# A linear-attention block and two MLPs on one core: the first block's attention in float32 products, wider query loads, and the lower parts on another engine

## The chip, the core and the metric

One Trainium2 chip, of which the program uses one core. Its engines run side by side, each in its own program order: TensorE (PE, with its weight loads as PEld), VectorE (DVE), ScalarE (ACT), GpSimd (POOL) and SyncE (SP), which here issues nearly all DMAs. The metric is the device time of one execution in microseconds (us); lower is better.

## The reference, cut to what matters

```python
# q, k, v: (8, 8, 576, 64) float32; g_norm: (64,) float32
kv  = einsum('bhsd,bhse->bhde', k, v)
out = einsum('bhsd,bhde->bhse', q, kv)
rms = sqrt(mean(out * out, axis=-1, keepdims=True) + 1e-06)
x   = out / rms * g_norm                 # then (B, S, H*D) = 4608 tokens x 512
x   = max(0.01 * (x @ w_in), x @ w_in) @ w_out          # 512 -> 2048 -> 512
return max(x @ moe2_w_in, 0) ** 2 @ moe2_w_out           # 512 -> 2048 -> 512
```

The four weights arrive as float64, read as pairs of 32-bit words.

## The kernel before

**Precision.** A float32 operand is split into an upper part, rounded to the engine's short float32 form (`F32R`, an ACT copy), and a lower part, the rest (a subtraction). A product of two split operands is three matmuls: upper x upper, upper x lower, lower x upper. A plain `F32` product is one call of the program; for it the trace has two matmul records.

**Blocks.** 4608 tokens are 9 blocks `j` of 512. Attention prepares the input of block `j` as four head pairs `p` of two 64-wide heads, each 128 partitions of `x`. A batch has 576 tokens, so block 0 lies in batch 0 and block 1 takes its first 64 tokens from it too. The steps of a pair:
- `kv` (`do_kv`, L338): k^T v for both heads from raw tiles, then the split into `kv_t`.
- `a` (`stage_a`, L376): four transposes of the raw queries, then the split (ACT L382, DVE L383).
- `b` (`stage_b`, L386): the product with kv (L396 to L398: three matmuls for each batch that the block touches), then square and copy (ACT L403, L404) and the split of the square (DVE L405, POOL L406).
- `s` (`stage_s`, L411): the mean of squares over a head, a product with a constant matrix `ones`, upper part (L414) and then lower part (L415).
- `c` (`stage_c`, L419): the reciprocal root (ACT L424, L425) and three DVE steps (L426, L429, L432); the last one also needs `gneg`, which comes from `g_norm` (`load_g`, L713).
- `d` (`stage_d`, L437): the split of x, upper by ACT L440, lower by POOL L441.

**First GEMM.** A slot is one `gemm1(j, m)` (L476): 12 matmuls of 128x512 on column group `m` of the first weight, 16 slots a block, 144 in all. `leaky` (L491) takes the result out of PSUM on ACT into a tile of a small pool (`hp`) and a DMA stores it. Weights are made from the raw words by `scale` (ACT L172, DVE L173 and L176), `join` (DVE L186 and L190) and `w` (`split_w`, ACT L202, POOL L203). Three are made in the prologue, the other 13 one a slot during block 0. From slot 20 on the other three weight matrices are made in the same way, split on POOL (L259) and stored.

**Order.** The program is a list written out by hand; each engine keeps to it. The prologue has attention of block 0 with a step for each pair; then, in each slot, weight work comes first, then the GEMM, then the attention steps of block `j+1`: pair `p` starts every four slots, `b` two slots behind `a`, `s` and `c` two further, `d` one further. The order inside a slot is `("s", "c", "b", "a", "d", "kv")`.

**Loads and buffers.** `pump` (L946) issues loads on SP's queue in the order in which the program will use them, as far as buffers allow: 8 units for raw k, v and weights (a pair of k and v counts 2), 3 raw query tiles. It runs once at the start and after each step that frees a buffer, so what it issues stands on SP's queue ahead of a DMA that a later step issues. `g_norm` is loaded on ACT's queue, in the step behind `a` and `kv` of the prologue's step 0. Big tiles take numbered slots (45) from a first-in-first-out list. PSUM has 8 banks; in the prologue `at_tile` goes round them, so its 16th tile, the mean of squares of pair 3, takes bank 0, which the first GEMM takes next.

**Afterwards** come the second GEMM of the first MLP and both of the second MLP (L608, L672), from operands and weights re-read from DRAM.

Of the kernel before, what the change touches and what calls it, by code (L numbers as in the profile page):

```python
# [10 lines left out]
F32 = mybir.dt.float32  # L11
# [7 lines left out]
def tile_linear_attention_two_mlps(  # L19
# [26 lines left out]
    nc = tc.nc  # L46
# [16 lines left out]
    TB = 512  # L63
    EPS = 1e-6
    LD_BUFS, Q_BUFS, KV_BUFS = 8, 3, 6
# [23 lines left out]
    NBIG = 45  # L89
# [7 lines left out]
    hp = ctx.enter_context(tc.tile_pool(name="hp", bufs=4))  # L97
# [225 lines left out]
    def load_kv(b, p):  # L323
        tiles = []
        for n, x in enumerate((k, v)):
# [3 lines left out]
            for r, c in SCH:  # L329
                nc.sync.dma_start(  # L330
# [7 lines left out]
    def do_kv(b, p):  # L338
# [22 lines left out]

    def load_q(i, p):
        a = qp.tile([P, TB // P, P], F32, tag="q", name=f"q_raw{i}_{p}")
        for r in range(TB // P):
            t0, o = i * TB + r * P, 0
            while o < P:
                b, s = divmod(t0 + o, S)
                n = min(P - o, S - s)
                nc.sync.dma_start(
                    out=a[o:o + n, r, :].rearrange("p (h d) -> p h d", h=2),  # L370
                    in_=q[b, 2 * p:2 * p + 2, s:s + n, :].rearrange("h s d -> s h d"),
                )
                o += n
        q_raw[i, p] = a

    def stage_a(i, p):  # L376
        a = q_raw.pop((i, p))
        ps = at_tile(TB, f"qtps{i}_{p}")
        for r in range(TB // P):
            nc.tensor.transpose(ps[:, r * P:(r + 1) * P], a[:, r, :], ident)  # L380
# [5 lines left out]
    def stage_b(i, p):  # L386
# [4 lines left out]
        while o < TB:  # L391
# [3 lines left out]
            c = slice(o, o + n)  # L395
            nc.tensor.matmul(out=ps[:, c], lhsT=t[:, 0, :], rhs=hi[:, c], start=True, stop=False)  # L396
# [14 lines left out]
    def stage_s(i, p):  # L411
        sqo, slot, sqs, slot2 = sq_t.pop((i, p))
        ps = at_tile(TB, f"ssps{i}_{p}")
        nc.tensor.matmul(out=ps, lhsT=ones, rhs=sqs[:, 0], start=True, stop=False)  # L414
        nc.tensor.matmul(out=ps, lhsT=ones, rhs=sqs[:, 1], start=False, stop=True)  # L415
        give_big(slot2)
# [20 lines left out]
    def stage_d(i, p):  # L437
# [3 lines left out]
        nc.gpsimd.tensor_tensor(out=xl, in0=osb, in1=f32(xh), op=ALU.subtract)  # L441
# [11 lines left out]
    def attention_steps(j, pace, a, b_, c, d):  # L453
# [5 lines left out]
        for p in range(NP):  # L459
# [7 lines left out]
            add(at0 + c, "s", j, p)  # L467
# [252 lines left out]
    with tc.manual_schedule():  # L720

        prog = [("const",), ("x", 0)]
        steps = attention_steps(0, 1, 0, 1, 2, 3)
        jobs = [(0, m, 0) for m in range(NM)]
        for at0 in (2, 3, 4):
# [4 lines left out]
        for u in sorted(steps):  # L730
            order = ("b", "a", "s", "c", "d", "kv", "gn", "scale", "join", "w")
# [15 lines left out]
        for w in ((0, 1), (1, 0), (1, 1)):  # L747
            z, (a, b, c) = ("S", ("A11", "A12", "A22")) if LEFT[w] == 0 else ("T", ("B11", "B21", "B22"))
            for n in range(NPAIR):
# [3 lines left out]
                for st in (  # L753
# [6 lines left out]
                    ])  # L760
        n0, n1 = NM + 4, NM * NB - 12
# [116 lines left out]
        for s in range(len(slots)):  # L878
# [5 lines left out]
            order = ("s", "c", "b", "a", "d", "kv")  # L884
# [15 lines left out]
        def drop_pairs(ps):  # L900
# [10 lines left out]
            "a": stage_a, "b": stage_b, "s": stage_s, "c": stage_c, "d": stage_d, "mlp": spare.clear,  # L911
# [26 lines left out]

        pump()
# [38 lines left out]
```

## Time and profile before

| | |
|---|---|
| time, median of 3 runs | 1647.82 us (1647.33 to 1648.06) |
| profiled execution: time | 1646.02 us |
| profiled execution: span, first to last instruction | 1644.2 us |
| first GEMM: first matmul, last matmul ends | 41.7 us, 559.4 us |
| first GEMM, block 0 ends | 109.2 us |
| PE busy over the span | 1586.1 us (96%) |
| DVE, ACT, POOL busy | 1219.0, 768.1, 254.9 us |

The times are from the span's start. A busy PE is not a PE at its peak, since matmuls overlap; where the speed matters, it is read from the distance between starts.

### The profile page before, as it was taken

What the parts mean: (1) busy time and instruction counts of PE and PEld (TensorE: products, weight loads), DVE (VectorE), ACT (ScalarE), POOL (GpSimd) and SP (SyncE); (2) the same over time, 40 slices, a digit from 0 to 9 for tenths busy, and PEclk for the clock granted to TensorE, in tenths of its full rate; (3) what the DMA queues carried; (4) which work ended last, traced back from release to release, by engine and by line L of the source; (5) the groups of instructions that cost most, each with busy time, mean ns of one, the idle gap of its engine ahead of it and who ended that gap; (6) DMA issues with size and microseconds to landing.
All of it is one profiled execution on the core that took longest, in us unless ns stands there. A gap on an engine that the chain in (4) does not pass through costs nothing. (4 is left out here: it accounts for less than half of the span.)

```text
span 1644.2 us, 27915 instructions
## 1 busy us (share of the span) xinstructions
PE 1586.1 (96%) x10504; PEld 1424.0 (87%) x10504; DVE 1219.0 (74%) x1867; ACT 768.1 (47%) x1439; POOL 254.9 (16%) x272
## 2 busy tenths in 40 slices
PE   4999999999999999999999999999999999999999
PEld 3778777777777899999999988888888999999999
DVE  5967777777775378888778888747877787777776
ACT  4566555665565334444444454424444444444443
POOL 3444454454554000000000000000000000000000
PEclk7999999999999999999999999999999999999999
DMA  8677989989987954444335645584449833333442
GB/s 217 197 200 251 322 280 284 314 287 305 328 283 245 407 183 135 135 133 135 129 129 180 230 160 170 182 289 153 161 157 318 334 132 129 129 131 135 134 129 84
DMA packets 249447, 338.45 MB, mean 206 GB/s; under 512 B 55264, under 2 KB 180192, under 8 KB 249312
## 3 DMA queue, kind: packets, MB, share of 16 engines
q1 hardware_dynamic: 249152, 336.67, 61.5%
q8 instruction: 83, 1.36, 0.3%
q14 instruction: 52, 0.43, 0.1%
q10 hardware_dynamic: 160, 0.00, 0.0%
HBM read 198.18 MB, written 138.41 MB: 205 GB/s over the span
## 5 line engine op out<-in xcount | busy, mean ns | idle before, releaser
L481 PE MATMUL hps<-xh,w 128*128 128x512 f32 x1152 | 374.7, 397 | 8.4 <-DVE sqo L426 6.2
L481 PEld LDWEIGHTS hps<-xh,w 128*128 128x128 f32 x1152 | 217.7, 189 | 56.9 <-DVE sqo L426 6.7
L481 PE MATMUL hps<-xl,w 128*128 128x512 f32 x576 | 226.4, 393 | 0.8 <-POOL xl L441 0.8
L481 PEld LDWEIGHTS hps<-xl,w 128*128 128x128 f32 x576 | 109.2, 190 | 23.1 <-POOL xl L441 1.9
L493 ACT ACTIVATE h<-hps 128x512 f32<-128x512 f32 x144 | 85.0, 592 | 32.7 <-DMA g<-h 27.5
L587 DVE TENSOR_TENSOR h_C<-aps,u 128x512 f32<-128x512 f32 x72 | 49.5, 688 | 54.6 <-PE aps L608 33.1
L173 DVE TENSOR_SCALAR w_raw<-w_raw 128x512 uint32<-128x512 uint32 x64 | 48.8, 762 | 32.4 <-ACT wt L172 32.3
L587 DVE TENSOR_TENSOR u<-bps,p 128x512 f32<-128x512 f32 x72 | 49.5, 687 | 25.9 <-ACT p L618 12.9
L426 DVE SCALAR_TENSOR_TENSOR sqo<-ssps,sqo 128x512 f32<-128x512 f32 x36 | 24.9, 691 | 55.9 <-ACT sqo L425 55.0
L406 POOL TENSOR_TENSOR sqs<-sqo,sqs 128x512 fp32r<-128x512 f32 x36 | 49.2, 1366 | 85.9 <-DVE sqs L405 79.7
L190 DVE SCALAR_TENSOR_TENSOR wt<-wt,w_raw 128x512 uint32<-128x512 uint32 x64 | 58.1, 907 | 2.2
L441 POOL TENSOR_TENSOR xl<-sqo,xh 128x512 fp32r<-128x512 f32 x36 | 48.4, 1345 | 60.5 <-ACT xh L440 51.5
L618 ACT ACTIVATE p<-aps 128x512 f32<-128x512 f32 x36 | 21.3, 591 | 71.7 <-PE aps L608 71.7
L176 DVE SCALAR_TENSOR_TENSOR w_raw<-w_raw 128x512 uint32<-128x512 uint32 x64 | 53.0, 827 | 2.2
L608 PE MATMUL aps<-op_B21h,w 128*128 128x512 f32 (+1 forms) x160 | 52.2, 375 | 1.5 <-ACT p L618 1.5
L608 PE MATMUL bps<-op_T4h,w 128*128 128x512 f32 (+1 forms) x160 | 51.2, 369 | 0.6 <-DVE u L587 0.6
L608 PE MATMUL aps<-op_B22h,w 128*128 128x512 f32 (+1 forms) x160 | 51.2, 369 | 0.4 <-DVE h_C L587 0.4
L608 PE MATMUL bps<-op_T3h,w 128*128 128x512 f32 (+1 forms) x160 | 51.0, 368 | 0.0
L608 PE MATMUL bps<-op_T2h,w 128*128 128x512 f32 (+1 forms) x160 | 51.0, 368 | 0.0
L608 PE MATMUL aps<-op_B11h,w 128*128 128x512 f32 (+1 forms) x160 | 51.0, 368 | 0.0
L608 PE MATMUL aps<-op_T1h,w 128*128 128x512 f32 (+1 forms) x160 | 51.0, 368 | 0.0
L625 ACT ACTIVATE h_C<-aps 128x512 f32<-128x512 f32 x36 | 21.6, 599 | 62.1 <-issue 31.1
(1408 smaller groups left out, 4193.5 us busy)
## 6 DMA issues: line engine op xcount, KB each, us to landing
g_raw<-g SPq DMA_DIRECT2D x144, 512.0 KB, 5.6
w<-w SPq DMA_DIRECT2D x84, 512.0 KB, 6.6
g<-h SPq DMA_DIRECT2D x144, 256.0 KB, 5.7
g<-h_C SPq DMA_DIRECT2D x144, 256.0 KB, 2.5
w_raw<-in_moe_w_in_dram SPq DMA_DIRECT2D x32, 512.0 KB, 6.2
w_raw<-in_moe_w_out_dram SPq DMA_DIRECT2D x32, 512.0 KB, 5.8
w<-whS SPq DMA_DIRECT2D x64, 256.0 KB, 5.3
x_raw<-x SPq DMA_DIRECT2D x32, 512.0 KB, 6.2
```

The costliest lines, as they stand in the source:

```text
L173: nc.vector.tensor_scalar(out=upper, in0=upper, scalar1=0x80000000, scalar2=None, op0=ALU.bitwise_and)
L176: nc.vector.scalar_tensor_tensor(out=lower, in0=lower, scalar=29, in1=upper, op0=ALU.logical_shift_right, op1=ALU.bitwise_or,)
L190: nc.vector.scalar_tensor_tensor(out=t, in0=t, scalar=3, in1=lower, op0=ALU.logical_shift_left, op1=ALU.bitwise_or,)
L406: nc.gpsimd.tensor_tensor(out=sqs[:, 1], in0=sqo[:, 0], in1=f32(sqs[:, 0]), op=ALU.subtract)
L426: nc.vector.scalar_tensor_tensor(out=z, in0=ps, scalar=EPS, in1=z, op0=ALU.add, op1=ALU.mult)
L441: nc.gpsimd.tensor_tensor(out=xl, in0=osb, in1=f32(xh), op=ALU.subtract)
L481: nc.tensor.matmul(out=ps, lhsT=w[:, wh, c * P:(c + 1) * P], rhs=x_t[j][xh, c // 2][0][:, c % 2, :], start=(c == 0 and y == 0), stop=(c == ...
L493: nc.scalar.activation(out=h, in_=h_ps.pop((j, m)), func=AF.Prelu, alpha=0.01)
L587: nc.vector.tensor_tensor(out=t, in0=x, in1=y, op=ALU.add)
L608: nc.tensor.matmul(out=ps[:, p], lhsT=w[:, wh, c, :], rhs=t[xh][:, c, :], start=(fresh and p == 0 and c == 0 and y == 0), stop=(p == len(p ...
L618: nc.scalar.activation(out=p1, in_=ps, func=AF.Copy)
L625: nc.scalar.activation(out=h, in_=ps, func=AF.Relu)
```

## The change

- In block 0, kv stays in plain float32 (`kvf`, copied out by DVE), the queries are not split, and L396 to L398 become one float32 product. The split of kv that block 1 still needs is made later (`kvs`, slot 0).
- In blocks 0 and 1 the mean of squares is one float32 product of the unsplit square.
- From block 2 on the product of the square's lower part moves to a step of its own, `t`, one slot behind `s`; `c` moves with it, and the whole chain starts a slot earlier. In a slot, `a` now comes in a slot ahead of `c`.
- x's lower part is made by DVE in place of POOL, and so is the lower part of the first weight up to slot 16 (`relieve`, step `lo`).
- A query tile holds four consecutive tokens a partition: one DMA per head and batch. Four query tiles in place of three, 10 load units in place of 8, 5 `hp` tiles in place of 4, 44 big slots in place of 45.
- In the prologue, v of pairs 1 to 3 of batch 0 is loaded on ACT's queue, and `g_norm` on SP's. Weights 0 to 2 come one to two steps later in the order. Constants are set in another order.

```diff
-    LD_BUFS, Q_BUFS, KV_BUFS = 8, 3, 6
+    LD_BUFS, Q_BUFS, KV_BUFS = 10, 4, 6
-    NBIG = 45
+    NBIG = 44
+    PLAIN_SS = 2
-    hp = ctx.enter_context(tc.tile_pool(name="hp", bufs=4))
+    hp = ctx.enter_context(tc.tile_pool(name="hp", bufs=5))
+    kvf, kvf_slot = take_big([P, NP, 2, P], F32, "kvf")
+    kvf_t = [kvf[:, p, 0] for p in range(NP)]
+    lo_engine = [nc.vector]
+    def relieve():
+        lo_engine[0] = nc.gpsimd
...
-        nc.gpsimd.tensor_tensor(out=hl[:, 1], in0=t, in1=f32(hl[:, 0]), op=ALU.subtract)
+        lo_engine[0].tensor_tensor(out=hl[:, 1], in0=t, in1=f32(hl[:, 0]), op=ALU.subtract)
...
-                nc.sync.dma_start(
+                (nc.scalar if n and b == 0 and p else nc.sync).dma_start(
...
+        if b == 0:
+            for h in range(2):
+                r = slice(h * D, (h + 1) * D)
+                nc.vector.tensor_copy(out=kvf_t[p][r, r], in_=ps[r, r])
+            return
...
+    def split_kv(p):
+        t = kv_t[p]
+        nc.scalar.activation(out=t[:, 0], in_=kvf_t[p], func=AF.Copy)
+        nc.vector.tensor_tensor(out=t[:, 1], in0=kvf_t[p], in1=f32(t[:, 0]), op=ALU.subtract)
+        if p == NP - 1:
+            give_big(kvf_slot)
...
     def load_q(i, p):
-        a = qp.tile([P, TB // P, P], F32, tag="q", name=f"q_raw{i}_{p}")
...
+        a = qp.tile([P, QT, 2, D], F32, tag="q", name=f"q_raw{i}_{p}")
+        o = 0
+        while o < TB:
+            b, s = divmod(i * TB + o, S)
+            n = min(TB - o, S - s)
+            for h in range(2):
                 nc.sync.dma_start(
+                    out=a[o // QT:(o + n) // QT, :, h, :],
+                    in_=q[b, 2 * p + h, s:s + n, :].rearrange("(t c) d -> t c d", c=QT),
                 )
+            o += n
...
-            nc.tensor.transpose(ps[:, r * P:(r + 1) * P], a[:, r, :], ident)
+        by_c = ps.rearrange("f (t c) -> f c t", c=QT)
+        for c in range(QT):
+            nc.tensor.transpose(by_c[:, c, :], a[:, c].rearrange("p h d -> p (h d)"), ident)
+        if i == 0:
+            t, slot = take_big([P, 2, TB], F32, f"qf{i}_{p}")
+            nc.scalar.activation(out=t[:, 0], in_=ps, func=AF.Copy)
...
+            if i == 0:
+                nc.tensor.matmul(out=ps[:, c], lhsT=kvf_t[p], rhs=hi[:, c], start=True, stop=True)
...
+        if i < PLAIN_SS:
+            sq_t[i, p] = (sqo, slot, None, None)
+            return
...
+        if i < PLAIN_SS:
+            nc.tensor.matmul(out=ps, lhsT=onesf, rhs=sqo[:, 0], start=True, stop=True)
+        else:
+            nc.tensor.matmul(out=ps, lhsT=ones, rhs=sqs[:, 0], start=True, stop=False)
+        ss_t[i, p] = (sqo, slot, ps, sqs, slot2)
+    def stage_t(i, p):
+        sqo, slot, ps, sqs, slot2 = ss_t.pop((i, p))
+        if sqs is not None:
+            nc.tensor.matmul(out=ps, lhsT=ones, rhs=sqs[:, 1], start=False, stop=True)
+            give_big(slot2)
         ss_t[i, p] = (sqo, slot, ps)
...
-        nc.gpsimd.tensor_tensor(out=xl, in0=osb, in1=f32(xh), op=ALU.subtract)
+        nc.vector.tensor_tensor(out=xl, in0=osb, in1=f32(xh), op=ALU.subtract)
...
-            nc.scalar.dma_start(
+            nc.sync.dma_start(
                 out=gneg[h * D:(h + 1) * D, :], in_=g_norm.rearrange("(d o) -> d o", o=1)
...
-        for at0 in (2, 3, 4):
+        for at0 in (3, 5, 6):
...
+        for p in range(NP):
+            put(0, "kvs", p)
+        put(NM, "lo")
...
-                at0, pace = (s - 4, 4) if j else (s, 4)
+                at0, pace = (s - 5, 4) if j else (s, 4)
-                lags = (2, 4, 5) if j else (1, 2, 3)
+                lags = (2, 4, 5, 6) if j else (1, 2, 2, 3)
...
-            order = ("s", "c", "b", "a", "d", "kv")
+            order = ("s", "t", "c", "b", "a", "d", "kv", "kvs")
```

## Rows read from the trace of the kernel before

**Rows 1.** Windows: us; busy (instructions) of PE, PEld, DVE, ACT, POOL; clock; DMA.
```profile
0.00:41.70 41.70, 18.31 (x116) 12.34 (x116) 22.86 (x38) 19.38 (x38) 13.93 (x24) 0.78 0.80 215
41.70:109.20 67.50, 63.08 (x351) 48.42 (x352) 59.83 (x88) 41.01 (x80) 33.14 (x23) 0.96 0.72 213
109.20:515.90 406.70, 385.85 (x2119) 309.46 (x2119) 290.66 (x462) 236.91 (x528) 199.88 (x215) 1.00 0.88 282
559.40:1644.20 1084.80, 1075.33 (x7729) 1018.06 (x7728) 837.88 (x1267) 458.60 (x769) 0.00 (x0) 1.00 0.49 170
```
**Rows 2.** Waits of PE's matmuls, 109.2 to 515.9: us in total, times, longest.
```profile
PE ssps L415 <- POOL sqs L406: 13.5, 19, 1.7
PE ops L397 <- DVE qhl L383: 5.9, 6, 1.9
```
**Rows 3.** Waits of PE's weight loads, 109.2 to 515.9.
```profile
PEld ssps L415 <- POOL sqs L406: 23.7, 23, 2.1
PEld ops L397 <- DVE qhl L383: 9.8, 12, 2.2
```
**Rows 4.** Timeline of PE from 300.5: start, us, instruction [idle before <- releaser].
```profile
300.88 0.39 PE L481 MATMUL hps<-xl,w 128*128 128x512 f32 x1
301.11 0.39 PE L481 MATMUL hps<-xh,w 128*128 128x512 f32 x1
301.39 0.50 PE L414 MATMUL ssps<-sqs,ones 128*128 128x512 f32 x1
302.85 0.51 PE L415 MATMUL ssps<-sqs,ones 128*128 128x512 f32 x1 [0.95 <-POOL sqs L406]
```
**Rows 5.** Timeline of SP's queue, the first 24 us.
```profile
0.73 0.94 SPq L330 DMA_DIRECT2D k_raw<-in_k_dram  x2
...
16.15 1.00 SPq L148 DMA_DIRECT2D w_raw<-in_moe_w_in_dram  x2
17.26 2.21 SPq L369 DMA_DIRECT2D q_raw<-in_q_dram  x4
```
**Rows 6.** Timeline of all engines, the prologue.
```profile
10.65 0.62 ACTq L715 DMA_DIRECT2D gneg<-in_g_norm_dram  x1
...
14.28 0.21 POOL L718 TENSOR_SCALAR gneg<-gneg 128x1 f32<-128x1 f32 x1 [10.94 <-DMA gneg<-in_g_norm_dram]
```
**Rows 7.** Timeline of PE, 16 to 120.
```profile
24.04 1.30 PE L380 MATMUL qtps<-ident,q_raw 128*128 128x128 f32 x4 [3.63 <-DMA q_raw<-in_q_dram]
...
41.73 0.80 PE L481 MATMUL hps<-xh,w 128*128 128x512 f32 x1 [6.17 <-DVE sqo L426]
```
**Rows 8.** Timeline of DVE, 26 to 46.
```profile
30.81 0.42 DVE L173 TENSOR_SCALAR w_raw<-w_raw 128x512 uint32<-128x512 uint32 x1
31.26 0.69 DVE L176 SCALAR_TENSOR_TENSOR w_raw<-w_raw 128x512 uint32<-128x512 uint32 x1
...
36.86 1.49 DVE L173 TENSOR_SCALAR w_raw<-w_raw 128x512 uint32<-128x512 uint32 x1
38.38 1.63 DVE L176 SCALAR_TENSOR_TENSOR w_raw<-w_raw 128x512 uint32<-128x512 uint32 x1
...
40.99 0.68 DVE L426 SCALAR_TENSOR_TENSOR sqo<-ssps,sqo 128x512 f32<-128x512 f32 x1
```
**Rows 9.** Groups of DVE, 41.7 to 109.2: count, busy us, mean ns, idle before.
```profile
L173 DVE TENSOR_SCALAR w_raw<-w_raw 128x512 uint32<-128x512 uint32 x13 | 13.0, 1000 | 1.3 <-ACT wt L172 1.3
L190 DVE SCALAR_TENSOR_TENSOR wt<-wt,w_raw 128x512 uint32<-128x512 uint32 x14 | 12.6, 900 | 0.5
```
**Rows 10.** Instructions on tile g_raw, 700 to 800: ns min/median/max.
```profile
L572 DVE TENSOR_TENSOR op_(4, 0)_B<-g_raw,op_(4, 0)_B x3: 682/683/686, 717.1 to 724.6; 128x512 fp32r<-128x512 f32 x3
```
**Rows 11.** Timeline of PE: one pair's float32 kv products, then two pairs'.
```profile
79.28 0.80 PE L344 MATMUL kvps<-v_raw,k_raw 128*64 128x64 f32 x20
...
96.30 1.39 PE L344 MATMUL kvps<-v_raw,k_raw 128*64 128x64 f32 x40
```
**Rows 12.** Windows: blocks 2 to 6 of the first GEMM; columns as in Rows 1.
```profile
165.10:461.70 296.60, 280.00 (x1579) 224.48 (x1578) 215.02 (x345) 173.68 (x391) 146.67 (x159) 0.99 0.95 304
```

More of the change, by code (lines that the diff above doesn't have):

```diff
@@ L63, in tile_linear_attention_two_mlps @@
     TB = 512
+    QT = TB // P
     EPS = 1e-6
-    LD_BUFS, Q_BUFS, KV_BUFS = 8, 3, 6
+    LD_BUFS, Q_BUFS, KV_BUFS = 10, 4, 6
     GSCALE = 2.0 ** -112
@@ L378, in stage_a @@
         ps = at_tile(TB, f"qtps{i}_{p}")
-        for r in range(TB // P):
-            nc.tensor.transpose(ps[:, r * P:(r + 1) * P], a[:, r, :], ident)
+        by_c = ps.rearrange("f (t c) -> f c t", c=QT)
[4 more added lines that the diff above has]
+            nc.scalar.activation(out=t[:, 0], in_=ps, func=AF.Copy)
+            qT[i, p] = t, slot
+            return
         t, slot = take_big([P, 2, TB], F32R, f"qhl{i}_{p}")
@@ L395, in stage_b @@
             c = slice(o, o + n)
+            if i == 0:
+                nc.tensor.matmul(out=ps[:, c], lhsT=kvf_t[p], rhs=hi[:, c], start=True, stop=True)
+                o += n
+                continue
             nc.tensor.matmul(out=ps[:, c], lhsT=t[:, 0, :], rhs=hi[:, c], start=True, stop=False)
@@ L413, in stage_s @@
         ps = at_tile(TB, f"ssps{i}_{p}")
-        nc.tensor.matmul(out=ps, lhsT=ones, rhs=sqs[:, 0], start=True, stop=False)
-        nc.tensor.matmul(out=ps, lhsT=ones, rhs=sqs[:, 1], start=False, stop=True)
-        give_big(slot2)
+        if i < PLAIN_SS:
[8 more added lines that the diff above has]
+            give_big(slot2)
         ss_t[i, p] = (sqo, slot, ps)
@@ L451, in tile_linear_attention_two_mlps, with attention_steps @@
     kv_done = set()
-    def attention_steps(j, pace, a, b_, c, d):
+    def attention_steps(j, pace, a, b_, s, c, d):
         steps = {}
@@ L466, in attention_steps @@
             add(at0 + b_, "b", j, p)
-            add(at0 + c, "s", j, p)
+            add(at0 + s, "s", j, p)
+            add(at0 + c, "t", j, p)
             add(at0 + c, "c", j, p)
@@ L702, in constants @@
     def constants():
-        nc.vector.memset(eps, EPS)
-        nc.scalar.activation(out=eps2, in_=eps, func=AF.Abs_reciprocal_sqrt)
         make_identity(nc, ident)
-        for t in kv_t:
-            nc.gpsimd.memset(f32(t), 0.0)
+        nc.vector.memset(kvf, 0.0)
         nc.gpsimd.memset(onesf, 0.0)
@@ L711, in constants @@
         nc.vector.tensor_copy(out=ones, in_=onesf)
+        for t in kv_t[NP:]:
+            nc.gpsimd.memset(f32(t), 0.0)
     def load_g():
         for h in range(2):
-            nc.scalar.dma_start(
+            nc.sync.dma_start(
                 out=gneg[h * D:(h + 1) * D, :], in_=g_norm.rearrange("(d o) -> d o", o=1)
@@ L722, in tile_linear_attention_two_mlps @@
         prog = [("const",), ("x", 0)]
-        steps = attention_steps(0, 1, 0, 1, 2, 3)
+        steps = attention_steps(0, 1, 0, 1, 2, 2, 3)
         jobs = [(0, m, 0) for m in range(NM)]
-        for at0 in (2, 3, 4):
+        for at0 in (3, 5, 6):
             w = jobs.pop(0)
@@ L730, in tile_linear_attention_two_mlps @@
         for u in sorted(steps):
-            order = ("b", "a", "s", "c", "d", "kv", "gn", "scale", "join", "w")
+            order = ("b", "a", "s", "t", "c", "d", "kv", "gn", "scale", "join", "w")
             prog += sorted(steps[u], key=lambda st: order.index(st[0]))
@@ L910, in tile_linear_attention_two_mlps @@
             "const": constants, "gn": load_g, "x": x_tiles, "kv": do_kv,
[L911 removed]
+            "a": stage_a, "b": stage_b, "s": stage_s, "t": stage_t, "kvs": split_kv, "lo": relieve, "c": stage_c, "d": stage_d, "mlp": spare.clear,
             "scale": scale_w, "join": join_w, "w": split_w, "g1": gemm1, "lk": leaky,
@@ L937, in pump @@
                 load[kind][0](*args)
+        nc.vector.memset(eps, EPS)
+        nc.scalar.activation(out=eps2, in_=eps, func=AF.Abs_reciprocal_sqrt)
         pump()
```

11 lines of the change are left out of this document (2 added, 9 removed).

## Prediction

> **What bounds the kernel now.** I read the windows by stage first. The reader is to see four regimes [rows 1]. Until 41.7 us PE is mostly idle and the DMA share is 0.80. In block 0 (67.5 us) PE is busy 63.1 and DVE 59.8, much of it stretched. From 109.2 to 515.9 PE idles 406.7 - 385.9 = 20.8 us. From 559.4 on PE idles 9.5 us of 1084.8, so the change has nothing to win there beyond those 9.5. All that can be won lies ahead of 516 us; the next views were the waits of PE and the timelines of PE, DVE and SP there.
>
> In the middle stretch two waits make up nearly all the loss: the product of the square's lower part waits for POOL, and the query product for DVE's lower part [rows 2, 3]. The pair at 301 us shows the first: neighbours start 0.23 us apart, this lower product starts 1.46 us behind the upper one, so 1.23 us are lost where PE's row counts 0.95 of idle time [rows 4]. PE's account is therefore too low, and the weight loads' account, which starts earlier, too high. I take the middle: (13.5 + 23.7) / 2 = 18.6 us for POOL, (5.9 + 9.8) / 2 = 7.9 us for DVE.
>
> In the prologue SP issues one DMA every 0.49 us (two in 0.94, four in about 2), and the last raw queries are only issued at 17.26, behind two weights [rows 5]; PE waits 3.63 us for them until 24.04, and the first GEMM waits 6.17 us for L426 of pair 3, which frees bank 0 [rows 7]. That L426 stands on DVE behind weight steps that took 1.49 and 1.63 us where the same ones took 0.42 and 0.69 [rows 8].
>
> **The middle stretch, step by step.** The step `t` gives POOL one more slot, at least 12 x 0.23 = 2.8 us [rows 4]; the longest wait now is 2.1 [rows 3], and two shorter slots ahead of it take back at most 0.5. All 18.6 us go, if POOL doesn't get later; it loses x's lower part, so it should not. The query wait: DVE now runs `a` a slot ahead of `c`, whose three steps stood ahead of the query's lower part and themselves wait for ACT. I take 5 of 7.9, both ends being 0 and 7.9. DVE gains 28 subtractions of 0.68 us [rows 10] = 19 us on 290.7 busy of 406.7 [rows 1]; its idle 116 us hide them; without that cover they cost 19. ACT's and SP's moves cost nothing here: ACT is busy 237 of 406.7 [rows 1], and SP issues fewer query DMAs. Sum: -23.6, up to -26.5.
>
> What is late next is DMA. In blocks 2 to 6 transfers fill 0.95 of 296.6 us, 282 us of all 16 engines [rows 12]; with the same transfers this part can't fall below about 282, a gain of 15. It holds five of the seven blocks in the stretch, so of 23.6 some 17 would fall there; I take 15 there and 3 from the rest, **-18**. If the wider query rows move in longer pieces the cap loosens to -26; if late loads and stores push back through ACT, it is nearer -8. Both ends stay in the range.
>
> **Prologue.** The good part: v of three pairs (6 DMAs) goes to ACT's queue at 0.6 us each [rows 6], 3.7 us at the start, when ACT has nothing else to do; a query tile takes 2 DMAs in place of 4. SP is through with k, v, q of block 0 after 18 DMAs, 0.73 + 18 x 0.49 = 9.6 us in place of 19.5. Then transfers bound: 3.41 MB at 215 / 0.80 = 269 GB/s full rate [rows 1] is 12.7 us, so the last queries land at about 16 to 18 us in place of 24.
>
> The bad part: `g_norm` moves from ACT's queue, where it landed by 14.28 [rows 6], to SP's, at its place in the program. Ahead of it `pump` has put four weights (two with the 10 units at the start, two when `kv` of pair 0 frees its units), block 1's first query tile and its k and v: 3.41 + 4 x 0.52 + 0.26 + 0.59 = 6.4 MB. Weights and the queries behind them now wait in one line on this queue [rows 5, 7], so `gneg` lands at about 2.5 + 6.4 / 0.269 = 26 us, 27 with POOL's step; at 215 GB/s it would be 32. DVE waits for it in L432 of pair 0. Behind that stand on DVE the float32 kv of pair 3, which PE's product of pair 3 needs, and all of `c` for pairs 1 to 3; ACT waits in `d` of pair 0.
>
> DVE's order from 27.3 on, at unstretched prices (0.68 to 0.75 for the `c` steps and subtractions, 1.1 for `scale` or `join`) [rows 8, 10]: L432 of pair 0 and kv (1.2), `c` of pair 1 (2.1), x lower 0 (0.7), `scale` 0 (1.1), a wait for ACT's root of pair 2, whose product stood behind PE's product of pair 3 (1.3), `c` of pair 2 (2.1), x lower 1 (0.7), `join` 0 (1.1), `c` of pair 3 (2.1), x lower 2 (0.7), `scale` 1 (1.1), lower part of weight 0 (0.7): 14.9 us, to 42.2. The first GEMM can start when L426 of pair 3 frees bank 0, near 38.3, but its third matmul needs the lower part of weight 0. So it flows from about 42, as now (41.73). Were `gneg` in time, the same list would begin near 21.5 and wait a little more for PE, and the GEMM would flow from about 34.
>
> A float32 product costs, by the kv burst, 1.39 - 0.80 = 0.59 us for five steps of 64 columns (the two heads side by side), 0.12 each, 0.94 for 512 columns [rows 11]. The lower bound is 0.46, two short matmuls, since the trace has two records. I take 0.94. In place of two short ones (0.46) it costs 0.48 more, in place of three (0.69) 0.25 more. In block 0's attention these lie on a chain that waits for `gneg` anyway; block 1's four cost 4 x 0.48 = 1.9 us of PE inside block 0. The Trainium skill, page "FP8 and Floating Point Precision", section TensorE Precision Notes, says that true FP32 takes four passes through the array, which speaks against this part; by it a product would be 4 x 0.23 = 0.92, nearly the row's value, and the four would cost 1.8 in place of 1.9.
>
> **Block 0.** DVE's price for a weight: 0.42 + 0.69 + 0.42 + 0.69 unstretched, plus 0.68 for the lower part, 2.9 us. Now L173 and L190 alone average 1.00 and 0.90 [rows 9], 0.8 above the unstretched two, because POOL works beside them; afterwards POOL has nearly nothing to do until slot 16. So DVE's work per weight stays about what it is, 59 us behind the first GEMM's start, and it does not become the bound by itself: 42.2 + 59 + 3 for the last slot = 104. PE: 67.5 less its waits (idle 4.4 by the rows; by the weight loads' account about twice that, so I take 6.9), plus 1.9: 62.5, to 104.7. Against 109.2 that is **-4.5**, between 0 (`gneg` at 32, five later: 109.7) and -13 (`gneg` in time: 34.0 + 62.5 = 96.5).
>
> The Trainium skill, page "SBUF — State Buffer", section Who interferes with whom, gives a rule for the stretching: a DVE instruction with two SBUF inputs, or in its two-port mode, and a POOL instruction that reads SBUF block each other. The trace agrees for L173 (0.42 alone, 1.49 beside POOL) [rows 8]. By that rule x's lower part on DVE will itself be blocked at times where POOL still works, behind 109 us.
>
> **Elsewhere.** Constants, the fifth `hp` tile and the fourth query tile: nothing on the path, since PE waits for none of them [rows 2, 3]. One big slot fewer: nothing, with the rival below.
>
> **Sum.** 1646.0 - 18 - 4.5 = 1623.5 for the profiled execution; the median stands 1.8 above it, so 1625.
>
> **Rivals.**
> 1. `gneg` is not late (a tiny transfer passes the others). For it: it landed 3 us behind its issue on ACT's queue. Against: what stands behind weights on SP's queue landed behind them. Then -13 - 18: 1617.
> 2. The middle gives little: DMA at 0.95, or DVE, which POOL blocks at 28 subtractions by up to 1.1 us each (as 1.49 against 0.42 [rows 8]), 30 us in all; then the query waits stay or grow. -5 there, -4.5 in block 0: 1638.
> 3. Slower: the ring of big slots. Raw operands of the last two passes are loaded into a slot when the FIFO list gives it; with 44 a load may start one take later, about one group of 12 short matmuls, 1.5 us. There are 72 groups of seven behind 559 us [rows 1]. PE idles only 9.5 us there, so loads now come in time; if the slack were under 1.5 us, 72 x 1.5 = 108 us at worst. It decides from 0.32 us a group on, 23 in all; 0.4 a group gives 1654.
> 4. Nothing: PE in the middle gains no more than transfers let it, because packets that crowd also get slower, so that the stretch keeps its length within 3 us, and `gneg` comes at 32: 0 - 2, 1646.
>
> **Chances.** Forecast 0.60 (own range 1616 to 1633), rival 1 0.14, rival 2 0.14, rival 3 0.06, rival 4 0.06. A measurement tells 0.2%, 3.3 us, from no change. Faster: 0.60 + 0.14 + 0.14 = 0.88; same 0.06; slower 0.06. The range from 1609 (rival 1 with the looser cap) to 1639 (rival 2) leaves out rivals 3 and 4 and the tails.
>
> **What would show it.** Right: no wait of the lower mean-of-squares product for POOL behind block 2; POOL's `gneg` step near 27 us, with DVE idle ahead of it in L432; the first GEMM near 42 and block 0's end near 104; DMA share near 1 in blocks 2 to 6; PE's idle time behind 559 us unchanged. Wrong: a first GEMM that flows before 37; new waits of the query product for DVE; matmuls of L672 that wait for operands.

## The result: 1.1% faster, most of it from one line

The changed kernel takes 1629.7 us (median of 4 runs, 1627.9 to 1631.1), the kernel before beside it 1647.6 (1645.4 to 1648.1): ratio 0.9891, 95% interval 0.9879 to 0.9903. The prediction was 1625, range 1609 to 1639.

The profiled execution of the changed kernel is the longest of its four, 1631.1 us with a span of 1629.0. Against the 1644.2 of before its span is 15.2 us shorter, while the medians differ by 17.9; the account by stage below is that of the spans. First the windows by stage of the changed kernel (columns as in [rows 1]); the last line is the counterpart of [rows 12].

```profile
0.00:40.20 40.20, 17.99 (x113) 9.87 (x113) 13.38 (x28) 16.30 (x28) 1.99 (x12) 0.85 0.98 230
40.20:109.40 69.20, 64.25 (x375) 49.95 (x375) 61.05 (x115) 44.10 (x87) 1.29 (x1) 0.94 0.75 217
109.40:499.90 390.50, 379.65 (x2099) 310.91 (x2095) 296.48 (x488) 236.78 (x526) 170.68 (x185) 0.99 0.91 291
543.50:1629.00 1085.50, 1076.26 (x7729) 1019.50 (x7728) 838.91 (x1268) 459.02 (x769) 0.00 (x0) 1.00 0.50 170
163.90:448.70 284.80, 275.70 (x1561) 226.02 (x1558) 218.86 (x362) 174.81 (x391) 128.69 (x139) 0.99 0.98 314
```

Against [rows 1]: block 0 ends at 109.4 where it ended at 109.2, so all that was gained in the prologue is given back by then. The middle stretch falls from 406.7 to 390.5. Block 8 is 43.7 in both, and the part behind it grows by 0.7. In blocks 2 to 6 the DMA share is 0.98 and the length 284.8.

The waits of PE's matmuls, and then of its weight loads, in that middle stretch of the changed kernel:

```profile
PE ssps L454 <- DVE sqs L442: 7.9, 3, 3.4
...
PE ops L431 <- DVE qhl L413: 1.0, 2, 0.7
```

```profile
PEld ssps L454 <- DVE sqs L442: 12.7, 8, 3.8
PEld ops L431 <- DVE qhl L413: 2.0, 3, 1.1
```

L454 is the upper product of the mean of squares (L414 before), L460 the lower one (L415), L431 the query product (L397). The wait for POOL of [rows 2, 3] is gone and the query wait nearly so. But the upper product, which waited for nothing before, now waits for DVE's cast of the square (L442).

The prologue of the changed kernel, from its timeline (SP's queue, POOL, DVE and PE):

```profile
25.61 1.16 SPq L760 DMA_DIRECT2D gneg<-in_g_norm_dram  x2
28.83 0.21 POOL L763 TENSOR_SCALAR gneg<-gneg 128x1 f32<-128x1 f32 x1 [26.29 <-DMA gneg<-in_g_norm_dram]
29.08 0.75 DVE L477 SCALAR_TENSOR_TENSOR sqo<-sqo,gneg 128x512 f32<-128x512 f32 x1 [8.23 <-POOL gneg L763]
30.34 2.04 PE L427 MATMUL ops<-qf,kvf 128*128 128x512 f32 x2 [9.41 <-DVE kvf L367]
...
40.18 0.76 PE L527 MATMUL hps<-xh,w 128*128 128x512 f32 x1 [4.86 <-ACT w L213]
...
43.13 0.69 DVE L214 TENSOR_TENSOR w<-wt,w 128x512 fp32r<-128x512 f32 x1
43.87 1.22 PE L527 MATMUL hps<-xh,w 128*128 128x512 f32 x2 [2.50 <-DVE w L214]
```

The reader is to see the chain that was predicted: `gneg` is late, DVE stands 8.23 us in the last step of `c` (L477), behind which the float32 kv of pair 3 stands (L367), and PE waits 9.41 us for that. The first GEMM starts at 40.18 but flows from 43.87, when its third matmul has the lower part of weight 0.

### The profile page after: what moved, and what is told of

It reads as the page before. It is cut to its first block, busy times and chain, and to the rows that moved or that the text cites. A ratio compares the mean times of both kernels' runs of the same rounds, so it can differ in the third digit from the quotient of the medians.

```text
span 1629.0 us, 27836 instructions
## 1 busy us (share of the span) xinstructions
PE 1581.8 (97%) x10500; PEld 1426.1 (88%) x10500; DVE 1218.0 (75%) x1912; ACT 768.8 (47%) x1435; POOL 181.5 (11%) x208
## 5 line engine op out<-in xcount | busy, mean ns | idle before, releaser
L527 PE MATMUL hps<-xh,w 128*128 128x512 f32 x1152 | 382.8, 400 | 10.1 <-ACT w L213 4.9
L443 POOL TENSOR_TENSOR sqs<-sqo,sqs 128x512 fp32r<-128x512 f32 x28 | 43.3, 1547 | 174.3 <-DVE sqs L442 151.5
L633 DVE TENSOR_TENSOR u<-ps,p 128x512 f32<-128x512 f32 x18 | 12.4, 691 | 51.7 <-ACT p L729 51.7
L685 DVE SCALAR_TENSOR_TENSOR h_C<-h_C 128x512 f32<-128x512 f32 x72 | 49.0, 681 | 0.0
L181 DVE SCALAR_TENSOR_TENSOR w_raw<-w_raw 128x512 uint32<-128x512 uint32 x64 | 47.3, 739 | 2.2
L195 DVE SCALAR_TENSOR_TENSOR wt<-wt,w_raw 128x512 uint32<-128x512 uint32 x64 | 44.3, 693 | 2.2
```

Source lines behind the costliest of these rows:

```text
L181: nc.vector.scalar_tensor_tensor(out=lower, in0=lower, scalar=29, in1=upper, op0=ALU.logical_shift_right, op1=ALU.bitwise_or,)
L195: nc.vector.scalar_tensor_tensor(out=t, in0=t, scalar=3, in1=lower, op0=ALU.logical_shift_left, op1=ALU.bitwise_or,)
L443: nc.gpsimd.tensor_tensor(out=sqs[:, 1], in0=sqo[:, 0], in1=f32(sqs[:, 0]), op=ALU.subtract)
L527: nc.tensor.matmul(out=ps, lhsT=w[:, wh, c * P:(c + 1) * P], rhs=x_t[j][xh, c // 2][0][:, c % 2, :], start=(c == 0 and y == 0), stop=(c == ...
L633: nc.vector.tensor_tensor(out=t, in0=x, in1=y, op=ALU.add)
L685: nc.vector.scalar_tensor_tensor(out=h, in0=h, scalar=0.0, in1=h, op0=ALU.max, op1=ALU.mult)
```

## Experiments

Theories after the result: (A) the middle's gain comes from the slot `t`, which gives POOL time; (B) it comes from x's lower part leaving POOL; and in the prologue, `g_norm` behind SP's loads costs what the rest of the prologue wins. Distances between starts of PE's matmuls, less the 10th percentile for the same pair of lines and shapes, give the loss at a place; "loss" below means that sum in the middle stretch. In the kernel before it is 18.2 us at the lower product and 6.6 at the query product; in the changed kernel 10.6 at the upper product, none at the lower, 1.7 at the query. The middle stretch runs from the first hps matmul of block 1 to that of block 8: 406.7 before, 390.4 in the changed kernel.

### g_norm on ACT's queue

```diff
-            nc.sync.dma_start(
+            nc.scalar.dma_start(
                 out=gneg[h * D:(h + 1) * D, :], in_=g_norm.rearrange("(d o) -> d o", o=1)
```

> The changed kernel, with the load of g_norm back on ACT's queue. Theory: in the changed kernel DVE stands 8.2 us in L477 for gneg (ready at 28.8), and all that follows to the first GEMM is DVE's list; with gneg ready at about 15 the list starts 7 to 8 us earlier, the first GEMM flows from about 36 in place of 43.9, block 0 ends near 102, and the time is 7 to 8 us below the changed kernel's (1622, ratio to the kernel before 0.984 to 0.985). Rival: the late queries and PE's cold float32 products bound the prologue anyway; then the GEMM flows from 41 or later and the time falls by less than 3 us (above 1626).

Measured: 1621.6 us (5 runs, 1618.0 to 1624.6), ratio 0.9845 (0.9829 to 0.9861), 8.1 us under the changed kernel. Its timeline:

```profile
10.70 1.70 ACTq L760 DMA_DIRECT2D gneg<-in_g_norm_dram  x2
...
15.71 0.21 POOL L763 TENSOR_SCALAR gneg<-gneg 128x1 f32<-128x1 f32 x1 [13.17 <-DMA gneg<-in_g_norm_dram]
...
34.51 1.22 PE L527 MATMUL hps<-xh,w 128*128 128x512 f32 x2 [2.50 <-DVE w L214]
```

`gneg` is there 13.1 us earlier, the GEMM flows 9.4 us earlier, block 0 ends at 99.5 in place of 109.4, and the middle stays (389.6). So the place of this load on SP's queue costs 8 to 10 us: shown.

### Without the slot t

```diff
-                at0, pace = (s - 5, 4) if j else (s, 4)
+                at0, pace = (s - 4, 4) if j else (s, 4)
-                lags = (2, 4, 5, 6) if j else (1, 2, 2, 3)
+                lags = (2, 4, 4, 5) if j else (1, 2, 2, 3)
```

> The changed kernel without the slot between the two products of the mean of squares: chain start, s, t and c are where they were before from block 2 on; all else stays. Theory: POOL's wait comes back to the lower product (18 us over the middle stretch before) and the query's lower part stands behind c again (7 us), while the new wait of the upper product for DVE's cast (10 us) goes: 10 to 15 us above the changed kernel, 1640 to 1645. Rival: the middle gained because POOL lost x's lower part (and stores got a fifth tile), not by the slot; then POOL is in time without it, and the time stays within 4 us of 1630.

Measured: 1627.7 us (4 runs), ratio 0.9882 (0.9869 to 0.9896), middle 391.1. Waits of PE's matmuls from 109 to 500:

```profile
PE ssps L460 <- POOL sqs L443: 6.3, 12, 0.9
PE ops L431 <- DVE qhl L413: 2.5, 5, 0.7
```

Theory A fell. Without the slot the wait for POOL is back, but at 6.3 us where it was 13.5 [rows 2], since POOL has less to do; and the upper product's loss falls from 10.6 to 0.3, the lower's comes back at 8.9. Beside the line that went to DVE the slot trades one for the other, at no gain.

### The upper product a slot later too

```diff
-                lags = (2, 4, 5, 6) if j else (1, 2, 2, 3)
+                lags = (2, 5, 5, 6) if j else (1, 2, 2, 3)
```

> The changed kernel with the upper product of the mean of squares a slot later too, next to the lower one (both three slots behind b). Theory: the new wait of the upper product for DVE's cast is only a matter of two slots against three; both products then find their operands, the 10 us go, POOL's wait does not come back: 8 to 10 us below the changed kernel, 1620 to 1622. Rival: the cast's delay is a sign that DVE or the DMA has no room; then what is taken off here comes back as waits of the query product, of the lower product or of x, and the time stays within 3 us of 1630.

Measured: 1631.4 us (5 runs), ratio 0.9902 (0.9887 to 0.9917), middle 390.9. Waits of PE's matmuls from 109 to 500:

```profile
PE ops L431 <- DVE qhl L413: 4.6, 10, 1.4
PE hps L527 <- ACT h L539: 3.3, 5, 1.3
PE ops L430 <- ACT qhl L412: 1.6, 3, 0.6
```

The loss at both products of the mean of squares is down to 0.5 us, and the stretch is no shorter: the query product waits again, and PE now waits for ACT to empty the GEMM's banks. Three orders of the same work gave 390.4, 391.1 and 390.9 us.

### x's lower part, both ways

Back to POOL in the changed kernel, and, in the kernel before, to DVE as the one edit:

```diff
-        nc.vector.tensor_tensor(out=xl, in0=osb, in1=f32(xh), op=ALU.subtract)
+        nc.gpsimd.tensor_tensor(out=xl, in0=osb, in1=f32(xh), op=ALU.subtract)
```

> The changed kernel with x's lower part back on POOL. Theory: the 0.68 us subtractions lie in idle time of DVE, so the cast's delay comes from c, which now stands in the slot ahead of b, and does not change: the middle stretch keeps its 390 us within 4, block 0 shortens or lengthens by less than 3. Rival: x's lower part on DVE is what makes the cast late: then the wait of the upper product (10 us) falls below 4 and the time by 5 or more.

> The kernel before with one part of the change: x's lower part by DVE. The slot of its own for the lower product gained nothing (the changed kernel without it is 2 us faster), and x's lower part back on POOL cost 10 us. New theory: POOL's relief is what the middle stretch gained by; alone it takes most of POOL's waits away: the stretch between block 0's end and block 8 falls from 406.7 us to 391 to 396, the time by 10 to 15 us (1632 to 1637). Rival: it needs the slot, the tiles or the queries as well; the stretch stays above 402 and the time above 1643.

Measured: back on POOL 1639.8 us (5 runs, 1638.5 to 1641.0), ratio 0.9953 (0.9940 to 0.9965), middle 398.1. Alone 1632.4 us (4 runs, 1631.1 to 1633.6), ratio 0.9907 (0.9892 to 0.9924), middle 397.1. This line is worth 10.1 us when taken away from the change and 15 us when added alone (9.5 and 12.9 by the spans of the profiles). Alone, its middle gives 9.6 us, and its block 0 ends 2.8 earlier (106.2); PE's wait of the lower product for POOL falls from 13.5 us [rows 2] to 4.1. Back on POOL, neither expectation came true: the middle grows by 7.7 us, and the upper product's loss rises from 10.6 to 15.0 us. The largest of the waits of PE's matmuls there from 109 to 500, among which none is for POOL:

```profile
PE ssps L454 <- DVE sqs L442: 11.8, 8, 3.4
```

So without this line the rest of the change still gives 8.6 us in the middle (406.7 to 398.1).

Groups in the middle stretch, of the kernel before (POOL's lower part of x, DVE's L190):

```profile
L441 POOL TENSOR_TENSOR xl<-sqo,xh 128x512 fp32r<-128x512 f32 x29 | 38.1, 1314 | 50.5 <-ACT xh L440 41.5 <-issue 4.7 <-DMA q_raw<-in_q_dram 4.2
...
L190 DVE SCALAR_TENSOR_TENSOR wt<-wt,w_raw 128x512 uint32<-128x512 uint32 x46 | 42.7, 928 | 1.6
L173 DVE TENSOR_SCALAR w_raw<-w_raw 128x512 uint32<-128x512 uint32 x46 | 32.3, 702 | 27.9 <-ACT wt L172 27.8
```

and of the kernel before with x's lower part on DVE:

```profile
L190 DVE SCALAR_TENSOR_TENSOR wt<-wt,w_raw 128x512 uint32<-128x512 uint32 x46 | 39.6, 861 | 1.6
L173 DVE TENSOR_SCALAR w_raw<-w_raw 128x512 uint32<-128x512 uint32 x46 | 25.4, 553 | 16.7 <-ACT wt L172 16.5
...
L441 DVE TENSOR_TENSOR xl<-sqo,xh 128x512 fp32r<-128x512 f32 x29 | 21.7, 748 | 16.2 <-ACT xh L440 13.8 <-POOL whT L259 2.2
```

1314 ns on POOL became 748 on DVE, and L173 and L190 became 10 us cheaper in sum. All that DVE does there is 290.1 us where it was 290.7 [rows 1], with 21.7 us more work in it, as the window of the middle shows:

```profile
106.20:503.30 397.10, 384.71 (x2120) 311.20 (x2119) 290.07 (x491) 237.92 (x528) 162.04 (x186) 0.99 0.90 290
```

### Fewer transfers in the middle

Three quarters of each stored tile of one later weight matrix are left out, and its GEMM reads another matrix's tiles, so the product of that matrix is not the reference's.

```diff
-        store(w2_d[w][slot][:, half], f32(t).rearrange("p h c f -> p (h c f)"), *slots)
+        part = TB // 4 if w == (1, 0) else TB
+        store(w2_d[w][slot][:, half, :part], f32(t).rearrange("p h c f -> p (h c f)")[:, :part], *slots)
...
-            nc.sync.dma_start(out=f32(t), in_=w2_d[w][slot])
+            nc.sync.dma_start(out=f32(t), in_=w2_d[(0, 1) if w == (1, 0) else w][slot])
```

> The changed kernel with three quarters of each store of the second MLP's first weight left out (its product reads the prepared tiles of another weight, so this part of the output is another): 56 stores of 64 KB in place of 256 KB, 11 MB less between about 250 and 390 us; every other instruction stays. Theory: the middle stretch now stands at what the transfers allow (blocks 4 and 5 take 59.5 and 60.6 us at a DMA share of 0.97 and 0.99); with 11 MB less, about 35 us of full rate, blocks 4 and 5 fall to 54 to 56 us each and the middle from 390.5 to 380 to 383. Rival: these blocks are long by that weight's own steps on DVE, ACT and POOL; then they stay within 2 us of 120 together.

Measured: one run of 1625.9 us, middle 385.2, where 380 to 383 was expected; the rival, which kept blocks 4 and 5 within 2 us of 120, fell too. Blocks 4 and 5, where the left-out stores fall, in the changed kernel and then here:

```profile
273.80:393.90 120.10, 112.47 (x642) 91.68 (x640) 87.49 (x149) 70.12 (x158) 51.31 (x57) 0.98 0.98 312
```

```profile
276.30:389.40 113.10, 110.70 (x647) 90.38 (x641) 87.21 (x148) 69.18 (x157) 50.94 (x57) 1.00 0.82 240
```

With the DMA share down from 0.98 to 0.82 these two blocks take 7.0 us less. What is gone with it are two long stalls. The changed kernel's timeline of PE around the first of them, and windows of the stall and of what follows it:

```profile
285.66 0.39 PE L527 MATMUL hps<-xh,w 128*128 128x512 f32 x1
289.02 0.51 PE L454 MATMUL ssps<-sqs,ones 128*128 128x512 f32 x1 [2.98 <-DVE sqs L442]
...
291.18 0.63 PE L527 MATMUL hps<-xl,w 128*128 128x512 f32 x1
291.60 1.05 PE L527 MATMUL hps<-xh,w 128*128 128x512 f32 x2
```

```profile
286.00:289.00 3.00, 0.05 (x1) 0.00 (x0) 1.21 (x4) 2.21 (x6) 1.40 (x2) 1.00 0.95 311
289.00:291.00 2.00, 1.98 (x26) 1.72 (x27) 1.48 (x2) 2.00 (x5) 1.96 (x2) 0.93 1.03 371
291.00:293.00 2.00, 2.00 (x6) 1.52 (x6) 1.93 (x4) 1.97 (x6) 0.48 (x1) 0.50 1.04 367
```

The stall has a second half. After 2.98 us without a matmul, and behind the transposes and the kv product that follow, the granted clock is 0.50, the lower of its two levels (1.2 of 2.4 GHz), and the GEMM's matmuls start 0.42 us apart, where [rows 4] have 0.23. A second stall of that kind stands at 388 us. In the whole middle 15 of the changed kernel's distances between two GEMM matmuls are over 0.35 us, 3.7 us more than at full speed; with fewer stores there are none, and no such stall.

### Sizes of buffers, and the query tile

Four `hp` tiles, eight load units, the old query tile (one token a partition), and the old query tile without the slot `t`, each against the changed kernel and each one run:

```diff
-    hp = ctx.enter_context(tc.tile_pool(name="hp", bufs=5))
+    hp = ctx.enter_context(tc.tile_pool(name="hp", bufs=4))
```

```diff
-    LD_BUFS, Q_BUFS, KV_BUFS = 10, 4, 6
+    LD_BUFS, Q_BUFS, KV_BUFS = 8, 4, 6
```

```diff
-        a = qp.tile([P, QT, 2, D], F32, tag="q", name=f"q_raw{i}_{p}")
+        a = qp.tile([P, TB // P, P], F32, tag="q", name=f"q_raw{i}_{p}")
...
+                nc.sync.dma_start(
+                    out=a[o:o + n, r, :].rearrange("p (h d) -> p h d", h=2),
+                    in_=q[b, 2 * p:2 * p + 2, s:s + n, :].rearrange("h s d -> s h d"),
```

> The changed kernel with four result tiles in place of five. Theory: the fifth tile is not on the path: the middle stretch stays within 2 us of 390.5, though ACT's waits for stores grow. Rival: with transfers full, a store that lands late holds ACT, and ACT the cast and the query; then the middle grows by 4 us or more.

> The changed kernel with the load buffers back at 8 in place of 9. Theory (what the middle stretch gained beyond the lower part on DVE, 397.1 to 390.4 us, came from loads that start earlier): middle 395 to 397 us, span 1634 to 1636. Rival (buffers of loads are not what ends any wait there): middle 388 to 392, span 1628 to 1631.

The "9" in that text is a slip for 10.

> The changed kernel with the old query tile: one token a partition and four query buffers, so the old number of query transfers. Theory (the grouped query tile brought the 6.7 us of the middle stretch that the lower part on DVE does not explain): middle 395 to 397 us, waits of the query product back at some 7 to 9 us. Rival (it brought nothing of its own): middle 388 to 392, query waits 2 to 4.

> The changed kernel without the extra slot and with the old query tile, one token a partition; both undone alone left the middle stretch at 391.1 and 392.9 us, against 390.4, while the kernel before with x's lower part on DVE as its one edit had 397.1. Theory (slot and query tile stand in for each other: either is enough to take out the query wait, and together they are the 6.7 us): middle stretch 395 to 398 us, query loss 7 to 9 us in the distances between starts. Rival (each is worth what it showed alone, 0.7 and 2.5): middle 391 to 394, query loss 3 to 5.

| | total us | middle us |
|---|---|---|
| changed kernel | 1629.7 | 390.4 |
| four `hp` tiles | 1630.4 | 387.8 |
| eight load units | 1625.7 | 387.4 |
| old query tile | 1635.2 | 392.9 |
| old query tile, no `t` | 1633.4 | 394.1 |

The fifth `hp` tile and the two more load units bring the middle nothing. With eight units, too, neither of the two long stalls is there and the clock is 1.00, with all transfers and a DMA share of 0.97 in blocks 4 and 5:

```profile
271.30:386.60 115.30, 111.06 (x642) 90.05 (x640) 85.42 (x147) 69.13 (x157) 50.48 (x57) 1.00 0.97 305
```

So the stalls don't need fewer transfers to go, and of the 5 us that fewer stores gave, 2 to 5 may be the transfers'. The grouped query tile is worth 2.5 us there on its own, and with the slot taken out as well 3.7, close to what the two gave one by one (0.7 and 2.5): nearer the rival's range than the theory's. These are one run each. The changed kernel and the two with `g_norm` on ACT's queue and the slot kept, whose middle is the same program, have 390.4, 389.6 and 389.7 us, so 0.7 us is noise and 2.5 is little above it. In the prologue the old tile has more DMAs to issue ahead of `g_norm` (issued at 28.00 against 25.61), and the GEMM flows 2.3 us later, at 46.1. With eight units `gneg` is ready at 27.4 in place of 28.8 and the GEMM flows 1.8 us earlier: block 1's first k and v, which the changed kernel issues ahead of `g_norm`, come behind it there.

### The weight's lower part on POOL, and a best version

With `g_norm` on ACT's queue, the lower part of the first weights on POOL again:

```diff
-    lo_engine = [nc.vector]
+    lo_engine = [nc.gpsimd]
```

> The changed kernel with g_norm on ACT's queue (as in the first experiment, 1621.6) and the first weight's lower parts on POOL from the start, as before the change. Theory: in block 0 DVE is the way of the weights (busy 61 of 69 us) and TensorE waits for the lower part; on POOL each of 16 lower parts takes 1.3 us beside DVE and gives DVE 0.69 back, at the price of DVE steps that POOL's reads hold up: block 0 changes by -4 to +1 us from 68.7. Rival, from the kernel before: POOL beside DVE stretches the weight steps (1.00 and 0.90 in place of 0.42 and 0.69), so block 0 gets longer by 3 us or more.

Measured: 1621.9 us (4 runs), ratio 0.9845 (0.9830 to 0.9861), the same as with it on DVE (1621.6). Both sides of block 0 in two windows, from the GEMM's flow to the last weight's lower part, first on DVE and then on POOL:

```profile
34.50:95.00 60.50, 57.98 (x337) 45.62 (x337) 55.35 (x106) 40.22 (x80) 1.29 (x1) 0.97 0.89 251
```

```profile
32.50:97.20 64.70, 60.90 (x338) 46.51 (x338) 57.06 (x95) 41.25 (x83) 21.88 (x16) 0.96 0.91 247
```

With 11 instructions fewer in the window (15 subtractions of 11.0 us gone, 4 others in it, since it is longer) DVE is busy 1.7 us more: POOL beside it stretches the rest by nearly what the subtractions cost. The GEMM flows 2 us earlier, since the prologue's DVE has less to do, and block 0's weights take 4.2 us longer. Block 0 as a whole, from its first matmul, is 1.7 us longer (70.4 against 68.7): more than the theory's range and less than the rival's 3.

`g_norm` on ACT's queue and no slot `t`:

> The changed kernel with g_norm on ACT's queue and without the extra slot between ones products and residual step. If the two places are independent (the prologue gives 8 us, the slot nothing): start of the GEMM's flow at 34.5 us, stretch from the end of block 0 to the last hps matmul of block 8 389 to 392 us, total 1619 to 1622, the same as with g_norm alone. If the slot still matters once the prologue is clear: 1617 or less, or 1625 or more.

Measured: 1619.4 us (5 runs, 1617.0 to 1620.1), ratio 0.9833 (0.9820 to 0.9847), the best of all; middle 389.3, clock 1.00 in it, no stall of PE over 1.8 us from start to start. As expected the two places are independent. Leaving out the slot was about 2 us better in both pairs (1629.7 and 1627.7, 1621.6 and 1619.4), inside the intervals each time.

## Why the prediction was right, and where it was wrong

**The sum: inside the range; its parts: all short in the same direction.** Forecast -18 and -4.5 on a profiled 1646.0. Measured in the spans: -16.3 in the middle, +0.4 up to block 0's end, +0.7 behind 543 us. That is 7.3 us less gain than forecast, 4.9 of it in block 0.

**Middle, the size: near the forecast, in part by luck.** Blocks 2 to 6 were said not to fall below about 282 us with the same transfers [rows 12]; they came to 284.8 at a share of 0.98. That the transfers are what holds it is not shown: with fewer stores, where transfers fill only 0.91 of the stretch, blocks 2 to 6 still take 279.6 us, and with eight load units and all stores 281.3. Three orders of the steps ended within 0.7 us of each other while the waits changed place. So it is in part luck that -18 came near -16.3: a gain put down mostly to the step `t` was cut to a floor that is not shown to hold.

**Middle, the cause: wrong step.** "The step `t` gives POOL one more slot ... All 18.6 us go" was right for that wait, and the gain was put down to it. The run without the slot has the same middle. About half of the gain comes from what the text mentioned only in passing, that POOL "loses x's lower part, so it should not" get later: it is 9.6 of the 16.3 us when made alone, and 7.7 are lost when it is undone. Freed of 1314 ns a pair, POOL delivers the square's lower part earlier without any slot (4.1 us of waits left of 13.5). With the line undone and the slot kept no wait for POOL is left either, so slot and line are two cures for the same wait, and the second adds nothing. The slot by itself was not run. What the prediction did not have is what is late next in the program's order: with `c` a slot behind `s`, DVE's steps of `c` and ACT's `whA` come ahead of the next square, and the upper product waits for DVE's cast. At 287 us the chain can be read from the timeline of ACT, DVE and POOL:

```profile
283.88 0.69 DVE L471 SCALAR_TENSOR_TENSOR sqo<-ssps,sqo 128x512 f32<-128x512 f32 x1 [4.20 <-ACT sqo L470]
...
286.79 0.42 ACT L269 ACTIVATE whA<-ws 128x256 fp32r<-128x256 f32 x1 [2.94 <-DVE ws L258]
...
287.89 0.59 ACT L436 ACTIVATE sqo<-ops 128x512 f32<-128x512 f32 x1
...
288.51 0.46 DVE L442 CAST sqs<-sqo 128x512 fp32r<-128x512 f32 x1 [1.76 <-ACT sqo L436]
```

DVE waits 4.20 us for ACT's root, ACT then 2.94 for DVE's `ws`, behind which stand `whS`, `h` and the next pair's square, and PE waits for its cast. Two such stalls, of 3.4 and 3.8 us from start to start, and the slow clock behind them (3.7 us in all) take what the slot saves at the lower product (8.9 us of loss without it). The kernels without the slot have no stall over 2.5 us from start to start.

The chain starts earlier still. Ahead of each of the two stalls ACT's copy of a prepared weight waits for a store to land:

```profile
281.50 0.42 ACT L269 ACTIVATE whA<-wt 128x256 fp32r<-128x256 f32 x1 [1.72 <-DMA w<-whS]
...
383.82 0.42 ACT L269 ACTIVATE whA<-wt 128x256 fp32r<-128x256 f32 x1 [2.73 <-DMA w<-whS]
```

In the middle ACT waits 10.5 us for such stores in the changed kernel, 4.8 with eight load units, 3.8 without the slot, 23.3 with x's lower part back on POOL, and not at all in the two kernels with 45 big slots (the one before, and the one with x's lower part on DVE alone). With fewer stores it is 9.8, at other steps, so not each such wait reaches PE. The load units and the slot `t` keep more of the big slots taken, so the ring of 44 is the likely reason that a copy meets a tile still being stored; no run changed the ring by itself, so this is not shown. The prediction did name stores that "push back through ACT", as the lower end of its range; it put "One big slot fewer" at nothing and looked for a cost of the ring only behind 559 us. Of the 6.7 us between the one line alone (397.1) and the whole change (390.4), the query tile and the slot together have 3.7 (394.1 without either); the `hp` tiles and the load units have nothing that shows. Each of these is one profile, with 0.8 us between profiles of one program; the other 3 us stay open.

**DVE's cost: the cover was not needed.** The 28 subtractions were priced at 19 us hidden in DVE's idle time. Alone they took 21.7 us at 748 ns (29 of them), and DVE's busy time did not grow. In the changed kernel they mean 881 ns and its busy time is 296.5, against 290.7: the stretching that rival 2 feared is 0.2 us each, not 1.1. The Trainium skill, page "SBUF — State Buffer", section Who interferes with whom, says that a DVE instruction with two SBUF inputs and a POOL instruction that reads SBUF block each other; the runs agree (L190, which has two inputs, 928 ns to 861 when POOL lost one such instruction a pair), and show the other side of it: moving such an instruction from POOL to DVE removes a pair that blocks.

**Prologue: right in mechanism, 1.7 us off in size.** `gneg` was forecast on POOL at about 27 us and was there at 28.8; the flow at 42.2 and it was 43.9; with `gneg` in time at 34 and it was 34.5. The issues of SP were forecast at 0.49 us each [rows 5], all of block 0's k, v and q by 9.6 us. The changed kernel's queue shows otherwise:

```profile
0.74 0.95 SPq L341 DMA_DIRECT2D k_raw<-in_k_dram  x2
...
12.82 1.22 SPq L393 DMA_DIRECT2D q_raw<-in_q_dram  x2
...
16.49 4.34 SPq L393 DMA_DIRECT2D q_raw<-in_q_dram  x4
```

Two issues take 0.95 us at the start and 1.1 to 2.4 later, four up to 4.34, so the last queries of block 0 are issued at 14, and `g_norm` itself only at 25.61, 3.2 us ahead of its use. So it was late on SP, not in the transfers behind its issue; but with eight load units it was issued at 19.5 and used at 27.4. That the bytes ahead of it set the time, on whichever side of the issue the wait lies, is likely and not shown.

**Block 0: mis-sized, and with it the -4.5.** "DVE's work per weight stays about what it is, 59 us ..., and it does not become the bound by itself: 42.2 + 59 + 3 ... = 104". From the flow to the last weight's lower part it took 61.0 us, and from there to block 1 4.5: 43.9 + 61.0 + 4.5 = 109.4. DVE is busy 55.3 of those 61.0 and PE 58.6, and in several slots the GEMM takes a lower part 0.05 us after DVE finished it: weights come just in time, so what DVE got in more work was paid. The stretched steps did get cheap, as the groups of DVE in block 0 show (L173 and L190 had 1000 and 900 ns in [rows 9]):

```profile
L214 DVE TENSOR_TENSOR w<-wt,w 128x512 fp32r<-128x512 f32 x16 | 11.7, 730 | 2.1 <-ACT w L213 1.7
...
L195 DVE SCALAR_TENSOR_TENSOR wt<-wt,w_raw 128x512 uint32<-128x512 uint32 x15 | 10.4, 693 | 0.5
L178 DVE TENSOR_SCALAR w_raw<-w_raw 128x512 uint32<-128x512 uint32 x15 | 6.3, 421 | 0.0
```

But the 11.7 us of lower parts ate it. Of the three items the start is 1.7 us late, the list 2.0 long and the tail 1.5. The -4.5 itself was taken from PE: 62.5 us from 42.2, as if its 6.9 us of waits would go. From the flow to block 1 it took 65.6, against 66.3 before: PE's waits for POOL's lower part gave way to waits for DVE's (L214), 3.6 us by the weight loads' account from 44.5 on where POOL's were 4.4. So the -4.5 became +0.4.

**Float32 products: right, 0.08 us dear.** In block 1's mean of squares one starts at 56.14 us, and the second GEMM matmul behind it at 57.23; less that first matmul's 0.23 us it takes 0.86, where 0.94 was forecast. Its two records start 0.43 us apart.

**Rivals.** Rival 3, the ring of 44 slots: the part behind 543 us has 1085.5 us against 1084.8, PE idles 9.2; nothing. Rival 1 (`gneg` not late) did not happen, and the run that made it happen gave 1621.6, against the 1617 forecast for it: the -13 was -9.5 (block 0 ends at 99.5), since the weights' list is the longer one there too. Rivals 2 and 4 did not happen.

## What to carry to other kernels

A small load that an early step needs belongs on a queue with nothing ahead of it: here two DMAs of 256 bytes behind the prefetch cost 8 us. Before adding a slot for a late engine, take work from that engine and see whether the slot still gains anything; each of the three orders tried here moved PE's waits to another engine and left the middle's length within 0.7 us. Where DVE and POOL both read two operands from SBUF, moving one such step from POOL to DVE can cost DVE nothing; count what the neighbours' steps get back.

## What the runs showed of the hardware that was not expected

- Two PE stalls of 3.4 and 3.8 us from start to start cost half as much again in clock (3.7 us): behind the first, after 2.98 us without a matmul, the granted clock stood at 0.50 between 291 and 293 us and the matmuls were 0.42 us apart in place of 0.23. Without the slot `t` (1627.7 and 1619.4 us), with no stall over 1.8 us, the middle's clock is 1.00. A shorter stall can be followed by the lower level too: in the kernel before one of 2.19 us from start to start ends at 384.87 us, with 0.51 granted behind it (the line below), while with eight load units one of 2.49 us that ends at 414.87 was not (1.00).

```profile
385.30:388.70 3.40, 3.40 (x12) 2.82 (x11) 3.16 (x4) 2.65 (x6) 1.43 (x2) 0.51 0.93 253
```

- Taking 15 subtractions, 11.0 us, from DVE left it busy 1.7 us more when POOL did them, with four other instructions more in the window (57.06 of 64.7 us against 55.35 of 60.5).
- SP's issues took longer once transfers were under way: two took 0.95 us at the start and four up to 4.34 us at 16 us. What slowed them is not shown.
